# Sums kept in banks over turned token orders, last queries moved, maxima by trees, norm sums by stationary ones

## The chip, the cores and the metric

The kernel runs on one core of one Trainium2 chip. The metric is the device time of the program in microseconds (us), the median of several runs. The profile is one further execution of the same program under the hardware profiler. The engines are named as the profile names them: PE is TensorE with its matmuls, PEld its weight loads, DVE is VectorE, ACT is ScalarE, POOL is GpSimd and SP is SyncE, whose queue issues the transfers.

## The reference

Three stages follow one another. `attn` has 4 batches of 8 heads with 576 tokens of 64 values, and 32 memory slots for each head:

```python
a = phi - np.max(phi, axis=2, keepdims=True)           # over the 576 tokens
a = np.exp(a); a = a / (np.sum(a, axis=2, keepdims=True) + 1e-09)
k_m = np.einsum('bhsm,bhsd->bhmd', a, k)
v_m = np.einsum('bhsm,bhsd->bhmd', a, v)
scores = scale * np.matmul(q, k_m.transpose(0, 1, 3, 2))
scores = scores - np.max(scores, axis=-1, keepdims=True)
attn = np.exp(scores); attn = attn / (np.sum(attn, axis=-1, keepdims=True) + 1e-09)
attn_out = np.matmul(attn, v_m)
...
x = attn_out.transpose(0, 2, 1, 3).reshape(2304, 512)
h = x @ w_in                                           # 512 -> 2048
x = (h * (1.0 / (1.0 + np.exp(-1.702 * h)))) @ w_out   # 2048 -> 512
...
rms = np.sqrt(np.mean(x * x, axis=-1, keepdims=True) + 1e-06)
xn = x / rms * rms_g
g = xn @ w_gate                                        # 512 -> 1536
out = (g * (1.0 / (1.0 + np.exp(-g))) * (xn @ w_val)) @ w_o2
```

## The kernel before, in words

**Passes.** The 2304 tokens go in two passes `pr` of two batches, 1152 tokens each. Tokens lie along the columns of the tiles and model channels along the 128 partitions, so x of a pass is `x2[pr]`, four tiles `e` of 128 channels by 1152 tokens (the profile calls them x_0 and x_1). Nearly every product is made of three matmuls on a high and a low part of each factor (names that end in h and l, or index 0 and 1 of a pair).

**Attention.** A unit is a batch with half of its heads. Its steps are `att_k1` (maximum of phi over the tokens, by one reduction on DVE) or `att_k1t` (the same by a tree of `tensor_tensor` maxima; batches 0 and 1 use it), `att_k2` to `att_k5` (exp, sums, `k_m` and `v_m`; `att_k3s` sums the exponentials), then `att_q1` to `att_q4` (scores, their maxima, exponentials and sums, and `attnT`). Batch 0 is laid out on 128 partitions, the others on 96; the stage tile of batch 0 is padded by a memset of 1152 columns.

**First MLP.** The hidden 2048 channels go in 8 groups `g` of 256 (`a_g1`, `a_g2`). `vm_part` multiplies `v_m` by the group's slice of `w_in` beforehand (tiles vm_0 to vm_3, two banks apiece); `a_g1` multiplies `attnT` by it, 288 tokens at a time (pg<-attnT,vm_3h), ACT applies the activation and POOL or DVE forms the low part (gr). `a_g2` multiplies by `w_out` (pg<-gr,a_outh), for a token tile `t` and each `e`, six matmuls into one PSUM bank. DVE then adds the bank to x2: x<-x,pg. The token tiles are 384 wide, and 288 wide only in the first two groups of the first pass. All groups run their tokens in rising order.

**Norm.** Per pass and per tile of 384 tokens: `norm_1` squares and adds on ACT and POOL (sq, then sr); `norm_2` sums over the channels by six matmuls of 128 columns with the squares as weights (bank pnm), takes a root of 3 columns on ACT and a reciprocal of 3 columns on DVE; `norm_3` spreads these over the partitions by three transposes (bank pnr) and an ACT copy to rb; `norm_4` multiplies the four tiles of x by rb and rg on DVE.

**Second MLP.** `s_g3` and `s_g4` make the three products by sums and differences of quarters, group b for the first pass and s for the second (tiles ps_A, ps_S, c, oacc). The first pass's norm and its part b are spread over the second pass of the first MLP, its tokens over the slots of that pass.

**What sets the order.** The steps are not issued where they are called. A class `Plan` records every operation, and a list scheduler inside it gives each engine its queue, with estimated costs (`cost`), due times (shifted for some steps by a table `HASTE`) and a table `OTHER` that names operations to move between DVE and POOL. Where it expects the PE to stand still before a matmul that takes a new bank, `fill` puts matmuls of the constant `ones_r` (512 or 128 columns) into that bank first, which are overwritten. `plan.issue` emits everything from one line, so the profile shows L644 for nearly all instructions. PSUM has 8 banks of 512 values for each partition (pool `ps`), shared by all uses.

```python
    def issue(self, tc):
        with tc.manual_schedule():
            for _, _, op in self.order():
                getattr(self.real[op.eng], op.name)(*op.args, **op.kw)
...
    kmiscp = pool("kmi", 1, strict=True)
    psp = pool("ps", 8, bass.MemoryType.PSUM, spare=2, ahead=4)
```

Of the kernel before, what the change touches and what calls it, by code (L numbers as in the profile page):

```python
# [10 lines left out]
F32 = mybir.dt.float32  # L11
# [105 lines left out]
class Plan:  # L117
# [12 lines left out]
        "a_g1 0 0 1": 19.4,  # L130
        "a_g1 0 1 1": 11.5,
        "a_g1 0 1 2": 21.4,
        "a_g1 0 3 0": 26.4,
        "a_g1 0 4 0": 21.9,
        "a_g1 0 5 0": 26.3,
        "a_g2 0 0 2": 16.5,
        "a_g2 0 0 3": 13.2,
        "a_g2 0 1 0": 9.5,
        "a_g2 0 2 0": 23.0,
        "a_g2 0 2 2": 27.6,  # L140
        "a_g2 1 5 1": 110.4,
        "att_k1 2 1": 45.4,
        "att_k2 2 1": 35.4,
        "att_k3 0 0": 96.8,
        "att_k5 0 1": 60.2,
        "att_k5 2 0": 7.8,
        "att_q1 2 1 0": 0.3,
        "att_q3 1 0 0": 43.2,
        "att_q3 1 0 1": 81.5,
        "att_q3s 2 1 0": 3.9,  # L150
        "att_q3s 2 1 1": 35.9,
        "att_q3s 3 0 0": 35.4,
        "att_q3s 3 0 1": 59.0,
        "att_q4 1 1 0": 43.7,
        "att_q4 2 0 0": 22.2,
        "att_q4 2 1 1": 4.4,
        "att_q4 3 1 1": 69.4,
        "ld_src 0 0 1": 71.5,
# [5 lines left out]
        "s_g3 0 7 2": 67.1,
        "s_g3 1 0 2": 116.4,
        "s_g3 1 11 1": 57.9,
        "s_g3 1 11 2": -61.0,
        "s_g4 0 0 5": 45.2,
        "s_g4 0 0 6": 52.3,
        "s_g4 0 1 4": 58.8,  # L170
        "s_g4 0 5 5": 80.4,
        "s_g4 1 4 2": 131.2,
        "s_g4 1 5 0": -73.1,
        "t_a 0 1": 70.9,
        "t_b 0 1": 59.7,
        "t_c 0 0": 31.9,
        "t_d 0 1": 42.8,
        "vm_part 0 5 0": 29.8,
        "w_conv a 0 0 in 1": 62.2,
        "w_conv c 5 gate 1": 36.4,  # L180
        "w_conv c 5 o2 0": 48.2,
        "w_load a 0 0 in 1": 81.8,
        "w_load a 0 1 out 1": 56.9,
        "w_load a 0 4 out 1": 55.7,
        "w_load a 0 5 in 1": 66.5,
        "w_load b 1 vg": 141.7,
        "w_load c 2 val 1": 115.6,
        "w_load c 3 val 0": 126.6,
# [208 lines left out]
    def cost(op):  # L397
# [17 lines left out]
        if op.eng == "POOL":  # L415
            two = op.name == "tensor_tensor"
            each = 0.00215 if two else 0.00104 if op.kw.get("op0") is ALU.mult else 0.00355
            if op.kw.get("op") is ALU.mult:
                each = 0.0016
            t = 0.05 + each * n + (0.1 if two else 0.0)  # L420
            return t, t + 0.05
# [226 lines left out]
def kernel(  # L648
# [285 lines left out]
    def ld_src(u, i):  # L934
        b, g = u
        x = (k, v, q)[i][b, 4 * g : 4 * g + 4]
        if u not in stage:
            stage[u] = big(f"stage{b}_{g}")
            if b < N9:
                V.memset(stage[u][:, 3456:4608], 0.0)  # L940
# [383 lines left out]
    def a_g1(pr, g, t):  # L1324
# [23 lines left out]
        if t == 3:  # L1348
            vm.pop((pr, g))
            if g == NA - 1:  # L1350
                attnT.pop(pr)

    def a_g2(pr, g, t, eng=A):
        w = width(pr, g)
        n = slice(t * w, (t + 1) * w)
        if pr not in x2:
            x2[pr] = big(f"x2_{pr}").rearrange("p (e n) -> p e n", e=NE)
# [3 lines left out]
        for e in range(NE):  # L1361
            es = slice(e * P, (e + 1) * P)
            ps = psum("pg2")
            i = 0
            for fc in range(2):
                for a, y in ((0, 0), (1, 0), (0, 1)):
                    PE.matmul(
                        ps[:, :w], lhsT=wo[a][:, fc, es], rhs=gr[fc][:, y, :w],
                        start=(i == 0), stop=(i == 5),
                    )  # L1370
                    i += 1
            if g == 0:
# [5 lines left out]
        if t == PT // w - 1:  # L1378
# [20 lines left out]
    def norm_2(pr, t):  # L1399
        sr = nrm.pop((pr, t))  # L1400
        ps = psum("pnm")
        for s in range(TB // P):
            c = slice(s * P, (s + 1) * P)
            for y in range(2):
                PE.matmul(
                    ps[:, c], lhsT=sr[:, y, c], rhs=ones_r, start=(y == 0), stop=(y == 1)
                )
        r = smp.tile([P, 2, 4], F32, tag="r", name="r")
        A.activation(
# [413 lines left out]
```

## Time and profile before

| | us |
|---|---|
| median of 3 runs | 847.02 (846.75 to 849.77) |
| the profiled execution, whole | 843.96 |
| the profiled execution, span of its trace | 842.2 |
| PE busy in the span | 827.5 (98%) |
| DVE busy | 655.1 (78%) |
| ACT busy | 494.0 (59%) |
| POOL busy | 296.4 (35%) |

The span runs from the first to the last recorded instruction; 1.76 us of the execution lie around it. The profiled execution is 3.06 us shorter than the median of the timed runs. A share of busy time is a mean over the whole span, and stages differ: DVE is busy nearly all the time in the first pass and less than half of it at the end.

### The profile page before, as it was taken

Reading aid. Unit: us, or ns where it says so; the run is one execution under the profiler, and the core shown is the slowest. Engines: PE = TensorE matmul, PEld = TensorE weight load, DVE = VectorE, ACT = ScalarE, POOL = GpSimd, SP = SyncE. Lnnn points to the kernel's source line nnn. Section 1 sums busy time; section 2 is a strip of 40 time slices with the busy share of each in tenths; the row PEclk is TensorE's granted clock in tenths of the full one; section 3 lists DMA queues with packets and bytes.
Section 4 is the critical chain, followed back from the end, with each engine's and each line's share of the span. In section 5 each row is a group of like instructions: output and inputs, shape, how many; then the busy total and the mean of one; then the engine's idle time right before and its main releaser. Section 6 shows DMA issues by size and latency. Waiting matters only on the chain.

```text
span 842.2 us, 16000 instructions
## 1 busy us (share of the span) xinstructions
PE 827.5 (98%) x5789; PEld 787.4 (93%) x5789; DVE 655.1 (78%) x1363; ACT 494.0 (59%) x1222; POOL 296.4 (35%) x295
## 2 busy tenths in 40 slices
PE   7999999999999999999999999999999999999997
PEld 6899999999999999999999999999999999999996
DVE  7978999999998998989989888767775435545555
ACT  4687878687778757666577755435552443323321
POOL 4444555666344556455846510120450000000000
PEclk9989999999999999999999999999999999999999
DMA  9964757856848776665676478463455543514314
GB/s 340 271 214 144 236 204 206 275 192 188 278 170 279 253 237 222 211 217 190 219 256 230 165 276 287 163 238 131 157 163 168 184 147 104 200 55 171 126 50 113
DMA packets 76767, 166.99 MB, mean 198 GB/s; under 512 B 7312, under 2 KB 29328, under 8 KB 76688
## 3 DMA queue, kind: packets, MB, share of 16 engines
q1 hardware_dynamic: 76688, 165.97, 59.5%
q8 instruction: 46, 0.75, 0.4%
q14 instruction: 33, 0.27, 0.1%
HBM read 106.69 MB, written 59.24 MB: 197 GB/s over the span
## 4 chain that ended last, share of the span: by engine, by line
PE 78%; DVE 10%; DMA 4%; issue 3%; ACT 3%; POOL 2%; SPq 0%; POOLq 0%; ACTq 0%; DVEq 0%
PE pg L644 42%; PE ps_A L644 21%; PE ps_S L644 9%; DVE pad L644 3%; PE pvm L644 2%; DVE x L644 2%; PE pq L644 2%; PE pk L644 1%; DMA stage<-in_q_dram 1%; DVE kmisc L644 1%; DVE stage L644 1%; DVE cv L644 1%; DMA stage<-in_v_dram 1%; DMA raw_c_gate<-in_moe_w_gate_dram 1%; DMA raw_a_out<-in_moe_w_out_dram 1%
## 5 line engine op out<-in xcount | busy, mean ns | idle before, releaser
L644 PE MATMUL pg<-gr,a_outh 128*128 128x384 f32 (+1 forms) x736 | 195.2, 334 | 0.8 <-POOL gr L644 0.6
L644 PEld LDWEIGHTS pg<-gr,a_outh 128*128 128x128 f32 x736 | 132.7, 188 | 2.4 <-POOL gr L644 2.0
L644 PE MATMUL pg<-gr,a_outl 128*128 128x384 f32 (+1 forms) x368 | 121.9, 331 | 0.0
L644 POOL TENSOR_TENSOR gr<-gf,gr 128x288 fp32r<-128x288 f32 (+2 forms) x118 | 83.8, 727 | 101.1 <-ACT gr L644 52.4
L644 PE MATMUL pg<-s_o,pp 128*128 128x512 f32 x432 | 114.0, 391 | 0.0
L644 ACT COPY c<-ps_A 128x320 f32<-128x320 f32 (+1 forms) x144 | 57.2, 399 | 93.7 <-PE ps_A L644 91.8
L644 DVE TENSOR_TENSOR x<-x,pg 128x384 f32<-128x384 f32 (+1 forms) x172 | 88.9, 535 | 11.0 <-PE pg L644 9.7
L644 DVE TENSOR_TENSOR oacc<-oacc,pg 128x512 f32<-128x512 f32 x90 | 61.7, 686 | 45.7 <-PE pg L644 44.9
L644 PEld LDWEIGHTS pg<-s_o,pp 128*128 128x128 f32 x432 | 79.0, 188 | 14.6
L644 PE MATMUL ps_A<-tba,s_A 128*128 128x320 f32 (+1 forms) x576 | 88.5, 296 | 0.0
L644 PEld LDWEIGHTS ps_A<-tba,s_A 128*128 128x128 f32 x576 | 81.9, 190 | 1.6
L644 DVE TENSOR_TENSOR c<-c,ps_S 128x320 f32<-128x320 f32 (+1 forms) x96 | 43.2, 452 | 37.6 <-PE ps_S L644 29.3
L644 PEld LDWEIGHTS pg<-gr,a_outl 128*128 128x128 f32 x368 | 69.1, 188 | 0.0
L644 ACT ACTIVATE gf<-pg 128x288 f32<-128x288 f32 x128 | 50.5, 412 | 31.1 <-PE pg L644 27.4
L644 ACT CAST gr<-gf 128x288 fp32r<-128x288 f32 (+2 forms) x184 | 59.2, 363 | 6.9 <-PE pg L644 4.3
L644 PE MATMUL pg<-s_o,tbd 128*128 128x512 f32 x216 | 61.1, 392 | 0.0
L644 DVE TENSOR_TENSOR c<-c 128x256 f32<-128x256 f32 (+1 forms) x86 | 39.3, 466 | 18.3 <-ACT c L644 16.6
L644 POOL TENSOR_SCALAR pad<-pad 128x512 f32<-128x512 f32 x20 | 41.2, 2062 | 19.9 <-ACT pad L644 19.7
L644 POOL TENSOR_SCALAR cv<-cv 128x512 f32<-128x512 f32 x20 | 44.1, 2210 | 8.1 <-ACT cv L644 6.5
L644 PE MATMUL ps_A<-tbc,s_S 128*128 128x256 f32 (+1 forms) x288 | 46.0, 297 | 0.0
L644 PE MATMUL ps_A<-tbd,s_A 128*128 128x320 f32 (+1 forms) x288 | 45.7, 297 | 0.1
L644 PE MATMUL ps_S<-tbb,s_S 128*128 128x256 f32 (+1 forms) x288 | 45.8, 296 | 0.0
(234 smaller groups left out, 1881.5 us busy)
## 6 DMA issues: line engine op xcount, KB each, us to landing
cache_s<-s_S SPq DMA_DIRECT2D x24, 512.0 KB, 3.7
s_S<-cache_s SPq DMA_DIRECT2D x24, 512.0 KB, 3.5
cache_b<-cv SPq DMA_DIRECT2D x36, 256.0 KB, 4.5
raw_a_in<-in_moe_w_in_dram SPq DMA_DIRECT2D x16, 512.0 KB, 5.3
raw_a_out<-in_moe_w_out_dram SPq DMA_DIRECT2D x16, 512.0 KB, 5.4
raw_c_gate<-in_moe_w_gate_dram SPq DMA_DIRECT2D x12, 512.0 KB, 4.7
raw_c_val<-in_moe_w_val_dram SPq DMA_DIRECT2D x12, 512.0 KB, 4.3
raw_c_o<-in_moe_w_out_dram SPq DMA_DIRECT2D x12, 512.0 KB, 4.4
```

Source lines behind the costliest of these rows:

```text
L644: getattr(self.real[op.eng], op.name)(*op.args, **op.kw)
```

## The change

Six edits come together. **Turned tokens and kept banks:** in the first MLP odd groups above 1 run their token tiles from 3 to 0 (`back`), so that two neighbouring groups meet at the same token tile. There the four banks of the earlier group are not closed, and the next group's matmuls add to them (`keeps`, `kept`); the four DVE additions of the earlier group go. **Half width in the second pass:** its first two groups also run 288 tokens at a time, slots `again`. **Queries of the last batch:** `att_steps` becomes `att_k` and `att_q`, and `att_q` of batch 3 runs at the start of the second pass (`last_side`). **Trees:** all units take `att_k1t`, and `att_k3s` goes to G (POOL). **Norm:** `norm_2` uses `ones_r` as the weights and the squares as the moving side, so that every partition holds the sums at once; root and reciprocal work on 384 columns, and `norm_3` is gone. **Memset:** the padding of the stage tile moves to POOL, with a cost for it in the planner. The tables `HASTE` and `OTHER` are replaced as a whole.

```diff
     HASTE = {
-        "a_g1 0 0 1": 19.4,
...
+        "a_g1 1 2 0": 114.4,
...
     OTHER = {
-        "a_g1 0 0 0": (17,),
...
+        "a_g1 0 0 0": (8,),
...
-                V.memset(stage[u][:, 3456:4608], 0.0)
+                G.memset(stage[u][:, 3456:4608], 0.0)
...
-    gt, x2 = {}, {}
+    gt, x2, kept, fresh = {}, {}, {}, set()
+    KEPT = range(NE)
+
+    def back(pr, g):
+
+        return g % 2 and g > 1
+
+    def keeps(pr, g, e):
+
+        return 1 < g < NA - 1 and e in KEPT
 
     def width(pr, g):
-        return HALF if (pr, g) in ((0, 0), (0, 1)) else TB
+        return HALF if g < 2 else TB
...
+        last = 0 if back(pr, g) else PT // w - 1
...
-            ps = psum("pg2")
-            i = 0
+            ps = kept.pop((pr, g, t, e), None)
+            i, keep = 0 if ps is None else 1, t == last and keeps(pr, g, e)
+            ps = psum("pg2") if ps is None else ps
             for fc in range(2):
                 for a, y in ((0, 0), (1, 0), (0, 1)):
                     PE.matmul(
                         ps[:, :w], lhsT=wo[a][:, fc, es], rhs=gr[fc][:, y, :w],
-                        start=(i == 0), stop=(i == 5),
+                        start=(i == 0), stop=(fc == 1 and (a, y) == (0, 1) and not keep),
                     )
                     i += 1
-            if g == 0:
+            if keep:
+                kept[pr, g + 1, t, e] = ps
+                fresh.add((pr, t, e)) if g == 0 else None
+            elif g == 0 or (pr, t, e) in fresh:
+                fresh.discard((pr, t, e))
                 copy(eng, acc[:, e, n], ps[:, :w])
...
     def norm_2(pr, t):
         sr = nrm.pop((pr, t))
         ps = psum("pnm")
-        for s in range(TB // P):
-            c = slice(s * P, (s + 1) * P)
-            for y in range(2):
-                PE.matmul(
-                    ps[:, c], lhsT=sr[:, y, c], rhs=ones_r, start=(y == 0), stop=(y == 1)
-                )
-        r = smp.tile([P, 2, 4], F32, tag="r", name="r")
-        A.activation(
-            out=r[:, 0, 0:3], in_=ps[:, 0:TB:P], func=AF.Sqrt, bias=epst, scale=1.0 / DM
-        )
-        V.reciprocal(out=r[:, 1, 0:3], in_=r[:, 0, 0:3])
-        nrm[pr, t] = r
-
-    def norm_3(pr, t):
...
-        A.copy(out=nrm[pr, t], in_=ps[:, :TB])
+        for y in range(2):
+            PE.matmul(ps[:, :TB], lhsT=ones_r, rhs=sr[:, y], start=(y == 0), stop=(y == 1))
+        r = kmiscp.tile([P, 1024], F32, tag="kmi", name="rb")
+        A.activation(out=r[:, :TB], in_=ps[:, :TB], func=AF.Sqrt, bias=epst, scale=1.0 / DM)
+        V.reciprocal(out=r[:, TB : 2 * TB], in_=r[:, :TB])
+        nrm[pr, t] = r[:, TB : 2 * TB]
...
-    def att_steps(u, k3, k3s, q1, q3s):
-        if u[0] < 2:
-            yield att_k1t, u, V
-        else:
-            yield att_k1, u
+    def att_k(u, k3):
+        yield att_k1t, u, V
         yield att_k2, u
         yield att_k3, u, k3
         if u[0] >= N9:
-            yield att_k3s, u, k3s
+            yield att_k3s, u, G
         yield att_k4, u
         yield att_k5, u
+
+    def att_q(u, q1, q3s):
...
+    def last_side():
+        for g in range(2):
+            yield from att_q((3, g), (A, A), (G, G))
...
-            side, per = pair_side(0), 1
+            side, per = last_side(), 2
...
-            line(a_g1, *key[1:], t)
+            turned = back(*key[1:])
+            line(a_g1, *key[1:], 3 - t if turned else t)
```

What the planner makes of it shows at two places. The first is DVE in the second pass of the first MLP, where the first norms of x_0 are made. Before, a norm's reciprocal has 3 columns (r) and stands between the low parts of vm_2:

```order
L644 TENSOR_TENSOR x_1_702<-x_1_702,pg_757 128x384
L644 TENSOR_TENSOR vm_2l<-pvm,vm_2h 64x256 x3
L644 RECIPROCAL r<-r 128x3
L644 TENSOR_TENSOR vm_2l<-pvm,vm_2h 64x256
L644 TENSOR_TENSOR gr<-gf,gr 128x192
```

In the changed kernel two reciprocals of 384 columns (rb) stand in the same queue, one ahead of the squares of the third token tile (sq_0_2), one between the low parts of vm_3:

```order
L605 RECIPROCAL rb<-rb 128x384
L605 TENSOR_TENSOR sq_0_2_790<-sq_0_2_790 128x384
L605 SCALAR_TENSOR_TENSOR x_0_211<-x_0_211,rg,rb 128x384 x2
L605 TENSOR_TENSOR x_1_661<-x_1_661,pg_781 128x288
L605 SCALAR_TENSOR_TENSOR x_0_211<-x_0_211,rg,rb 128x384 x2
L605 TENSOR_TENSOR x_1_661<-x_1_661,pg_809 128x384
L605 TENSOR_TENSOR vm_3l<-pvm,vm_3h 64x2x256
L605 RECIPROCAL rb<-rb 128x384
L605 TENSOR_TENSOR vm_3l<-pvm,vm_3h 64x2x256
L605 SCALAR_TENSOR_TENSOR x_0_211<-x_0_211,rg,rb 128x384 x3
L605 TENSOR_TENSOR x_1_661<-x_1_661,pg_810 128x384
L605 SCALAR_TENSOR_TENSOR x_0_211<-x_0_211,rg,rb 128x384
```

The reciprocal, its width and the multiplications by rb have moved ahead of vm_3l, whose last four pieces come in the row behind these. The second place is PE at the start, in the attention of batches 0 and 1 (stage_0, stage_1; pq are its banks, pvm those of vm_part). Before, the fills with ones_r go into a bank of vm_part:

```order
L644 MATMUL pk_217<-ident,mx 96x128
L644 MATMUL pq_140<-twin,stage_0_115 128x64 x3
L644 MATMUL pvm<-ones_r 128x512 x9
L644 MATMUL pvm<-ones_r 128x128 x2
L644 MATMUL pvm<-wide,vlh_131 128x256
```

In the changed kernel they stand ahead of the scores' transposes of batch 0 (pq_140), and ahead of the sums of batch 1 (pk_190):

```order
L605 MATMUL pq_153<-stage_1_117 64x2x32 x4
L605 MATMUL pq_153<-stage_1_117 64x32 x4
L605 MATMUL pq_140<-ones_r 128x512 x18
L605 MATMUL pq_140<-ones_r 128x128
L605 MATMUL pq_140<-twin,stage_0_115 128x64 x3
L605 MATMUL pk_190<-ones_r 128x512 x2
L605 MATMUL pk_190<-ones_r 128x128
```

Nineteen fills now precede pq_140, and the matmuls of vm_part (wide) have left this place.

## Rows read from the trace of the kernel before

**Rows 1.** The page: the span and the busy time by engine.

```profile
span 842.2 us, 16000 instructions
PE 827.5 (98%) x5789; PEld 787.4 (93%) x5789; DVE 655.1 (78%) x1363; ACT 494.0 (59%) x1222; POOL 296.4 (35%) x295
```

**Rows 2.** Windows: stretch, length, busy PE, PEld, DVE, ACT, POOL; clock; DMA.

```profile
0.00:47.00 47.00, 40.30 (x402) 35.30 (x403) 38.12 (x99) 28.33 (x69) 19.17 (x27) 0.94 1.01 312
40.00:50.00 10.00, 9.03 (x55) 8.74 (x56) 6.60 (x19) 6.45 (x19) 4.64 (x4) 0.66 0.99 295
60.00:240.00 180.00, 177.84 (x1421) 172.18 (x1421) 169.87 (x351) 138.53 (x338) 96.14 (x91) 1.00 0.69 223
240.00:411.00 171.00, 170.21 (x1113) 169.33 (x1112) 155.74 (x302) 117.37 (x288) 96.48 (x100) 1.00 0.66 218
411.00:490.00 79.00, 78.86 (x523) 74.53 (x522) 69.19 (x130) 56.59 (x125) 47.33 (x42) 1.00 0.60 204
```

**Rows 3.** Timeline of PE: start, length of a run of instructions, what it is.

```profile
282.09 0.34 PE L644 MATMUL pg<-gr,a_outh 128*128 128x384 f32 x1
282.27 0.49 PE L644 MATMUL pnr<-ident,r 128*128 128x128 f32 x3
282.51 0.42 PE L644 MATMUL pg<-gr,a_outh 128*128 128x384 f32 x1
...
428.32 0.78 PE L644 MATMUL pnm<-ones_r,sr 128*128 128x128 f32 x6
428.94 1.81 PE L644 MATMUL ps_A<-tbd,s_A 128*128 128x320 f32 x12
```

**Rows 4.** Groups on DVE by form: busy us, mean ns | idle before, releaser.

```profile
L644 DVE TENSOR_TENSOR x<-x,pg 128x384 f32<-128x384 f32 x156 | 81.8, 544 | 9.6 <-PE pg L644 8.4
L644 DVE SCALAR_TENSOR_TENSOR x<-x,rg,rb 128x384 f32<-128x384 f32 x24 | 15.6, 680 | 0.5 <-ACT rb L644 0.5
L644 DVE TENSOR_REDUCE kmisc<-kmisc 96x128 f32<-96x768 f32 x8 | 12.1, 1518 | 0.0
L644 DVE TENSOR_TENSOR x<-x,pg 128x288 f32<-128x288 f32 x16 | 7.1, 448 | 1.4 <-PE pg L644 1.3
L644 DVE TENSOR_TENSOR y<-kmisc 96x384 f32<-96x384 f32 x3 | 2.3, 759 | 0.0
L644 DVE TENSOR_TENSOR kmisc<-kmisc,y 96x128 f32<-96x128 f32 x3 | 0.9, 284 | 0.0
L644 DVE MEMSET stage<- 128x1152 f32 x2 | 2.0, 1018 | 0.3 <-issue 0.2
L644 DVE RECIPROCAL r<-r 128x3 f32<-128x3 f32 x6 | 0.9, 168 | 0.8 <-ACT r L644 0.8
L644 DVE RECIPROCAL stage<-stage 128x12 f32<-128x12 f32 x2 | 0.5, 228 | 0.3
```

**Rows 5.** Groups on POOL by form.

```profile
L644 POOL TENSOR_SCALAR pad<-pad 128x512 f32<-128x512 f32 x20 | 41.2, 2062 | 19.9 <-ACT pad L644 19.7
L644 POOL MEMSET kz<- 128x192 f32 x8 | 2.3, 282 | 7.9 <-PE pk L644 7.9
```

**Rows 6.** What PE waited for, by window: us in total, times, longest.

```profile
PE pvm L644 <- DVE a_inl L644: 0.8, 1, 0.8
...
PE pg L644 <- POOL gr L644: 0.6, 1, 0.6
PE pnr L644 <- DVE r L644: 0.2, 1, 0.2
```

**Rows 7.** Timeline of PE at the start.

```profile
33.18 2.38 PE L644 MATMUL pvm<-ones_r 128*128 128x512 f32 x11
...
47.01 0.83 PE L644 MATMUL pg<-attnT,vm_0h 128*128 128x288 f32 x2
...
55.58 0.42 PE L644 MATMUL pg<-gr,a_outh 128*128 128x288 f32 x2
55.84 0.29 PE L644 MATMUL pg<-gr,a_outl 128*128 128x288 f32 x1
```

More of the change, by code (lines that the diff above doesn't have):

```diff
@@ L129 @@
     HASTE = {
-        "a_g1 0 0 1": 19.4,
[L131 to L146, printed above, removed]
@@ L164 @@
[L164 to L180, printed above, removed]
@@ L181 @@
[L181 to L188, printed above, removed]
+        "a_g1 1 2 0": 114.4,
+        "a_g2 0 1 1": 112.8,
+        "a_g2 0 1 2": 93.7,
+        "a_g2 0 3 1": 53.1,
+        "a_g2 0 3 2": 61.7,
+        "a_g2 0 4 0": 39.7,
+        "a_g2 1 6 0": 122.4,
+        "a_g2 1 7 0": 106.9,
@@ new lines @@
+        "att_q1 2 1 1": 84.7,
+        "att_q3 1 0 1": 314.7,
+        "att_q3 2 1 0": 60.8,
+        "att_q3 3 0 1": 174.3,
+        "ld_phi 0 1": 652.0,
+        "norm_4 0 2 2": 123.4,
+        "norm_4 0 2 3": 132.3,
+        "s_g3 0 11 2": 194.1,
+        "s_g4 1 2 2": 222.6,
+        "s_g4 1 5 4": 243.3,
+        "s_g4 1 5 5": 95.7,
+        "s_g4 1 5 6": 95.0,
+        "s_g4 1 5 8": 77.2,
+        "t_b 0 0": 53.9,
+        "t_b 0 1": -44.6,
+        "t_c 0 0": 31.4,
+        "vm_part 0 1 0": 124.4,
@@ L189 @@
+        "w_conv a 0 6 in 0": 82.9,
+        "w_conv c 1 o2 1": 100.3,
+        "w_conv c 5 val 0": 133.4,
     }
     OTHER = {
[1 row of a table removed]
[1 row of a table added]
         "a_g1 0 0 2": (8,),
[12 rows of a table removed]
[10 rows of a table added]
         "a_g1 0 4 0": (17,),
[3 rows of a table removed]
[3 rows of a table added]
         "a_g1 0 5 2": (19, 21),
[19 rows of a table removed]
[20 rows of a table added]
         "a_g1 1 4 2": (8, 10, 19, 21),
[3 rows of a table removed]
[2 rows of a table added]
         "a_g1 1 5 3": (17,),
[3 rows of a table removed]
[6 rows of a table added]
         "att_k3 1 0": (2,),
@@ L416, in cost @@
             two = op.name == "tensor_tensor"
-            each = 0.00215 if two else 0.00104 if op.kw.get("op0") is ALU.mult else 0.00355
+            each = 0.00215 if two else 0.00104 if op.name == "memset" or op.kw.get("op0") is ALU.mult else 0.00355
             if op.kw.get("op") is ALU.mult:
@@ L1347, in a_g1 @@
                 sub_lo(G, gr[:, 1, d], gf[:, c0:c1], gr[:, 0, d])
-        if t == 3:
+        if t == (0 if back(pr, g) else 3):
             vm.pop((pr, g))
@@ L1377, in a_g2 @@
                 )
-        if t == PT // w - 1:
+        if t == last:
             wt.pop(("a", pr, g, "out"))
@@ L1401, in norm_2 @@
         ps = psum("pnm")
-        for s in range(TB // P):
-            c = slice(s * P, (s + 1) * P)
-            for y in range(2):
-                PE.matmul(
-                    ps[:, c], lhsT=sr[:, y, c], rhs=ones_r, start=(y == 0), stop=(y == 1)
-                )
-        r = smp.tile([P, 2, 4], F32, tag="r", name="r")
-        A.activation(
-            out=r[:, 0, 0:3], in_=ps[:, 0:TB:P], func=AF.Sqrt, bias=epst, scale=1.0 / DM
-        )
-        V.reciprocal(out=r[:, 1, 0:3], in_=r[:, 0, 0:3])
-        nrm[pr, t] = r
-    def norm_3(pr, t):
-        r = nrm.pop((pr, t))
-        ps = psum("pnr")
-        for s in range(TB // P):
-            PE.transpose(
-                ps[:, s * P : (s + 1) * P], r[:, 1, s : s + 1].to_broadcast([P, P]), ident
-            )
-        nrm[pr, t] = kmiscp.tile([P, 1024], F32, tag="kmi", name="rb")[:, :TB]
-        A.copy(out=nrm[pr, t], in_=ps[:, :TB])
+        for y in range(2):
[4 more added lines that the diff above has]
+        nrm[pr, t] = r[:, TB : 2 * TB]
     def norm_4(pr, t, e):
@@ L1622, in do @@
         at(*step)
-        plan.keen = step[0] in (norm_1, norm_2, norm_3, norm_4)
+        plan.keen = step[0] in (norm_1, norm_2, norm_4)
         step[0](*step[1:])
@@ L1653, in att_side @@
             yield ld_unit, u
-            yield from att_steps(u, G, V, (A, A), (G, G))
+            yield from att_k(u, G)
+            if u[0] == 2:
+                yield from att_q(u, (A, A), (G, G))
+    def last_side():
+        for g in range(2):
+            yield from att_q((3, g), (A, A), (G, G))
     def norm_side(pr):
@@ L1674, in weights, with unit @@
         conv(hf)
-    def unit(u, k3, q3s):
-        for step in att_steps(u, k3, G, (A, A, A) if u[0] < N9 else (A, A), q3s):
+    def unit(u, k3, q3s=None):
+        for step in att_k(u, k3) if k3 else att_q(u, (A, A, A) if u[0] < N9 else (A, A), q3s):
             do(step)
     first = [("a", 0, g, t) for t2 in (0, 2) for g in range(2) for t in (t2, t2 + 1)]
+    again = [("a", 1, *x[2:]) for x in first]
     slots = first + [
@@ L1684 @@
         for key in groups[2:]
+        if key not in (("a", 1, 0), ("a", 1, 1))
         for t in range(4 if key[0] == "a" else 3)
     ]
+    j1 = 4 * NA
+    slots[j1:j1] = again
     at_slot = {0: halves(groups[1])[:2], 1: halves(groups[1])[2:]}
@@ L1691 @@
             continue
-        nxt = halves(groups[2] if j < 8 else groups[i + 1])
+        nxt = halves(groups[2] if j < 8 else groups[NA + 2] if j1 + 4 <= j < j1 + 8 else groups[i + 1])
         if key[0] == "a":
-            at_slot.setdefault(j, []).extend(nxt[j % 4 : j % 4 + 1])
+            if j1 <= j < j1 + 2:
+                nxt = halves(groups[NA + 1])
+                at_slot.setdefault(j, []).extend(nxt[2 * (j - j1) : 2 * (j - j1) + 2])
+            elif not j1 + 2 <= j < j1 + 4:
+                at_slot.setdefault(j, []).extend(nxt[j % 4 : j % 4 + 1])
             if key[1]:
-                at_slot[j] += [later.pop(0)]
+                at_slot.setdefault(j, []).append(later.pop(0))
         else:
@@ L1716 @@
     for g in range(2):
-        unit((0, g), V, (G, G))
+        unit((0, g), V)
+        unit((0, g), None, (G, G))
     for hf in outs:
@@ L1733 @@
             for g in range(2):
-                unit((1, g), G, (G, G))
-            for g in range(2):
-                for c in range(2):
-                    line(vm_part, 0, g, c, 1)
+                unit((1, g), None, (G, G))
+            for c in range(2):
+                line(vm_part, 0, 0, c, 1)
             side = att_side()
+        if j == j1 + 4:
+            for step in side:
+                do(step)
+            side, per = pair_side(0), 2
         if key == ("a", 1, 0) and t == 0:
@@ L1747 @@
             if pr:
-                for step in islice(pair_side(1), 7 * NTB, None):
+                for step in islice(pair_side(1), 6 * NTB, None):
                     do(step)
@@ L1759 @@
         if j == 1:
+            for g in range(2):
+                unit((1, g), G)
+        if j in (1, j1 + 1):
             for c in range(2):
-                line(vm_part, 0, 1, c, 0)
-        nxt = groups[2] if j == 6 else groups[i + 1] if j > 7 and t == 2 and i + 1 < len(groups) else None
+                line(vm_part, j // j1, 1, c)
+        nxt = groups[2] if j == 6 else groups[NA + 2] if j == j1 + 6 else None if j1 <= j < j1 + 8 else groups[i + 1] if j > 7 and t == 2 and i + 1 < len(groups) else None
         if nxt and nxt[0] == "a":
@@ L1782 @@
         elif t:
-            late = [(a_g2, *key[1:], t - 1)]
+            late = [(a_g2, *key[1:], 3 - t if turned else t - 1)]
         for step in islice(side, per + (j % 4 == 1) if j else 0):
```

18 lines of the change are left out of this document (removed), and 214 rows, old and new, of the table OTHER.

## The prediction

> **What bounds the kernel now.** I read the page first. PE is busy for 827.5 of 842.2 us, every other engine for less than four fifths [rows 1]. The time can therefore fall in two ways only: PE gets fewer or shorter instructions, or the 14.7 us in which it stands still shrink. The windows say where these are. From 0 to 47 us, attention ahead of the first `a_g1`, PE is busy 40.30 of 47.00; from 60 to 240 us, the first pass of the first MLP, it misses 2.16; from 240 to 411, the second pass, 0.79; from 411 to 490, the start of part b, 0.14 [rows 2]. The rest lies in the tail, which the change does not touch. The same windows show who is near the bound behind PE: DVE, busy 169.87 of 180 us in the first pass, 155.74 of 171 in the second, 69.19 of 79 in b. The view of waits names what PE waited for longest: in the first pass a low part made by DVE (0.8 us), in the second a low part by POOL (0.6 us) and the norm's r by DVE (0.2 us) [rows 6]. So a microsecond less of DVE is not a microsecond of time; in the first pass at most the 2.16 us can be had.
>
> One stretch has another limit. Between 40 and 50 us the granted clock is 0.66, a mean of the two levels 1.2 and 2.4 GHz, while it is 1.00 in all windows from 60 us on [rows 2]. PE had been feeding itself fills at 33.18 [rows 7] and then took short matmuls with waits between them. What a full clock would give there is at most (1 − 0.66) × 10 = 3.4 us.
>
> **The norm's matmuls.** I take distances between starts as the price, since matmuls overlap. Six pnm matmuls take 428.94 − 428.32 = 0.62 us, three pnr transposes 282.51 − 282.27 = 0.24 [rows 3]: 0.86 for each norm. The new form is two matmuls of 384 columns; one takes 282.27 − 282.09 = 0.18 [rows 3], so 0.36. Six norms save 6 × 0.50 = 3.0 us of PE work, and the wait of 0.2 us for r goes with the transposes: **−3.2**. This is work on the bounding engine, which nothing can hide; I take ± 0.5.
>
> **Fewer additions.** A kept group boundary saves four DVE additions; there are five in each pass, so 20 × 0.544 = 10.9 us [rows 4] in each. The trees replace 8 reductions of 1518 ns by 24 `tensor_tensor`; with 759 + 284 and one more of about 284 that is 1.33 us against 1.52 [rows 4], 1.5 us less in all. Batch 3's queries leave the first pass. With the mean of each group of the trace for every instruction of the queue, DVE's work between the first and the last addition to x_0 goes from 176 to 159 us. Over some 180 us that is a share of 0.88, below the 0.91 (155.74 of 171) at which the second pass misses only 0.79. Of the 2.16 us that PE misses I take **−2.0** (bounds 0, if the misses are POOL's, and −2.2). With it go the fills that the planner had put into a late bank of batch 3, two of 512 columns and one of 128; eleven fills take 2.38 us at the start [rows 7], so **−0.5** (0 to −1).
>
> The kept banks have a price that no row shows: from the last token tile of a group to the first of the next, four of the eight banks are held, and `a_g1` runs on the others. If PE then waited each time as it waited once for gr, 0.6 us [rows 6], ten boundaries would cost 6 us. The banks' readers, ACT's activations and DVE's additions, follow PE closely and DVE has fewer additions just there, so I take 0 (0 to +6).
>
> **Half width.** In the second pass 144 matmuls of 384 columns become 192 of 288, equally many columns. Two of 288 take 55.84 − 55.58 = 0.26 [rows 7], so 192 × 0.13 = 25.0 against 144 × 0.18 = 25.9. I take **+0.3** (−0.9 to +0.7, for 48 more instructions and weight loads). The 16 more additions cost DVE 16 × 0.448 us [rows 4] and 12 of 0.544 go.
>
> **The start.** Two memsets of 1.02 us leave DVE [rows 4]. On POOL one takes longer: 282 ns for 192 columns [rows 5], so some 1.7 us for 1152, and the two stand in the queue in which each pad costs 2.06 us [rows 5]. `att_q` of batch 1 and part of `vm_part` move behind the first `a_g1`. Nineteen fills stand ahead of pq_140; eleven took 2.38 us before [rows 7], so these take about 4. They delay nothing that is ready, but show where the planner expects PE to wait, and for POOL. Against the 6.7 us missed and the fills that are there now [rows 2, 7], I take **−1** (−5, if the half clock goes too, to +3, if POOL is late).
>
> **The reciprocals.** Six `reciprocal` of 3 columns at 168 ns become six of 384 columns. The trace has none so wide. From 3 to 12 columns the time goes from 168 to 228 ns [rows 4], 6.7 ns a column; carried on to 384 that is 0.168 + 381 × 0.0067 = 2.7 us. From below, an addition of 384 columns takes 0.544 [rows 4], and a reciprocal won't be faster. Between them I take the slope, rounded to 2.5, because it is measured on the operation itself. The order shows what stands behind: in the second pass one lies ahead of the squares of the third tile, so the third pnm comes later; the next lies amid the low parts vm_3l, and with seven multiplications of 0.68 us behind it [rows 4], so the last vm_3l, which the `a_g1` of the group's turn wants, comes some 2 × 2.3 = 4.6 us later. DVE's work in the second pass, by the same sum as above, goes from 154 to 161 and with three reciprocals to 168 us, while PE's part grows by some 5 us that it loses in the first pass (the moved queries). That makes DVE as busy as it was in the first pass before, where PE missed 2.16. I take **+3** (0 if the reciprocal is short or covered, +7 if all of the delay shows). In b three more lie within a stretch in which DVE has 79 − 69.19 = 9.8 us free [rows 2] and needs 3 × 2.3 = 7 of them: **+0.7** (0 to +4).
>
> The Trainium skill, page "VectorE: DVE Perf Modes", section "First, the fixed hardware budget", says that Reciprocal is an iterative divide with a repeat count of 8; at the 0.96 GHz of its "Specifications" that would be, as an estimate, 8.3 ns a column and 3.2 us for 384. The sum would be about 1 us worse by it in the second pass and 1 us in b. The measured slope of 6.7 ns stands nearer to that than to one column a cycle.
>
> **Sum.** −3.2 − 2.0 − 0.5 + 0.3 − 1.0 + 3.0 + 0.7 = −2.7 us, so the profiled 843.96 would become 841.3. The median of the runs is 847.02, 3.06 us above the profiled one; I put the same difference on the median: 844.3, rounded to **844**. Half a per cent, 4.2 us, is about what a measurement can tell from no change; the likeliest case is inside of it.
>
> **Rivals.**
> - *The reciprocal is covered or short.* PE loses nothing for it, so the +3.0 and the +0.7 fall out: 847.0 − 6.4 = 840.6. For it speaks that only 0.79 us are missed in the second pass now, and that a planner with due times may have left room; against it, 155.74 of 171 us of DVE.
> - *The start gains as well.* The half clock at 40 to 50 us goes (−3.4) on top of that or of a part of it: 836 to 838. For it, fills stand ahead of pq_140 and keep PE going; against it, more work for POOL at a place where PE waits.
> - *No change that can be told.* The additions were all hidden, and the norm's 3 us are given back by the reciprocals or the held banks: 846.5 to 848.
> - *Slower: the reciprocals.* At 2.5 us six cost DVE 14 us more. If all six stand in PE's way, the sum is −6.4 + 14 = +7.6, or 854.6; with five sixths of it, 852. It ends on the slower side of no change once more than 6.4 us of the 14 show, and of 0.5% once 10.6 do. For it speaks that three stand in the second pass ahead of work that PE wants within the same group, and three in b with 9.8 us free; against it, that b's first matmuls can go on with the token tiles already normed.
>
> **Chances.** The sum's own case, 840.5 to 847.5, has 0.36; the covered reciprocal 0.22; the start as well 0.11; no change 0.15; slower 0.16. Faster than 842.8 are the second and third, and about a fifth of the first: 0.40. Slower than 851.2 is most of the last and a little for held banks: 0.17. Within it 0.43. The range leaves out the lower part of the start's case and the upper one of the reciprocals': 836.5 to 851.5. The sum's own range is 840.5 to 847.5.
>
> **What would show it.** The reciprocals of rb have a row with their mean: 2.5 us by me; below 1 us the first rival holds. PE's view of waits in the second pass should name DVE, at vm_3l, or the third pnm, with 1 to 4 us; if POOL's gr or DVE's x appear at the turns of groups, the held banks are the cost. pnm must show 12 matmuls of 384 columns 0.18 apart and no pnr. PE's missing time from 60 us to the end of the first pass should fall below 1 us; if it stays at 2, DVE was not what PE waited for. The first `a_g1` against 47.01 and the clock between 40 and 50 us tell of the start. Wrong I would be if the second pass and b lose more than 8 us, or if the start moves by more than 4.

## The result, and the profile after

The changed kernel takes 856.28 us (median of 5 runs, 852.9 to 857.45) against 846.75 us of the kernel before beside it: 1.0098 times as long, 95% interval 1.0071 to 1.0124. It is slower by 9.5 us; 844 and no measurable change were forecast, and the range ended at 851.5. The profiled execution took 857.45 us, 13.5 more than that of before. The two profiles lie at opposite ends: before's is 3.06 us below its median, the changed kernel's is the longest of its five, so they show about 4 us more of a loss than the medians do.

The page of the changed kernel, which answers to [rows 1]:

```profile
span 855.6 us, 15960 instructions
PE 831.6 (97%) x5799; PEld 788.3 (92%) x5799; DVE 659.0 (77%) x1372; ACT 489.4 (57%) x1204; POOL 261.4 (31%) x256
```

PE is busy 4 us longer in a span 13.4 us longer. The windows of the stretches of [rows 2], with the same columns:

```profile
60.00:240.00 180.00, 175.20 (x1389) 170.22 (x1389) 165.21 (x342) 132.37 (x332) 92.74 (x95) 1.00 0.67 214
240.00:411.00 171.00, 165.55 (x1138) 162.47 (x1137) 156.97 (x301) 117.18 (x282) 80.65 (x72) 1.00 0.64 215
411.00:490.00 79.00, 75.41 (x481) 71.68 (x480) 64.74 (x120) 52.83 (x116) 37.00 (x40) 0.98 0.63 209
```

PE misses 4.80, 5.45 and 3.59 us, 13.84 in all, where it missed 2.16, 0.79 and 0.14, 3.09 in all. That is 10.75 of the 13.4 us by which the span grew; the first product with vm_0 comes 2.26 us later, at 49.27 instead of 47.01. What PE waited for, from the view of waits of these three stretches (us in total, times, longest):

```profile
PE pg L605 <- ACT gf L605: 1.9, 3, 1.0
PE pk L605 <- DVE kmisc L605: 1.1, 1, 1.1
...
PE pg L605 <- ACT gf L605: 2.0, 3, 1.3
PE pg L605 <- DVE vm_3l L605: 1.6, 1, 1.6
PE pnm L605 <- POOL sr L605: 0.9, 1, 0.9
...
PE ps_S L605 <- DVE c L605: 1.2, 1, 1.2
PE ps_A L605 <- ACT s_S L605: 1.2, 1, 1.2
PE ps_A L605 <- POOL s_A L605: 0.7, 1, 0.7
```

(The names s_A, s_S and c are sums and differences that part b multiplies; sr is the sum of squares that pnm takes.) Two things are new. Products into pg wait for gf, ACT's activation that frees a bank, in both passes. And in the second pass and b, PE waits for work that stands behind DVE's reciprocals. Their group on DVE by form, beside the additions that answer to [rows 4]:

```profile
L605 DVE TENSOR_TENSOR x<-x,pg 128x384 f32<-128x384 f32 x104 | 54.8, 546 | 5.2 <-PE pg L605 4.7
L605 DVE RECIPROCAL rb<-rb 128x384 f32<-128x384 f32 x6 | 15.3, 2547 | 0.7 <-ACT rb L605 0.6
```

52 additions of 384 columns are gone, 16 of 288 have come with the half width, and six reciprocals of 2.55 us. DVE's timeline at the second of them:

```profile
308.56 2.54 DVE L605 RECIPROCAL rb<-rb 128x384 f32<-128x384 f32 x1
311.02 0.62 DVE L605 TENSOR_TENSOR vm_3l<-pvm,vm_3h 64x512 fp32r<-64x512 f32 x1
311.56 1.66 DVE L605 SCALAR_TENSOR_TENSOR x<-x,rg,rb 128x384 f32<-128x384 f32 x3
313.15 0.54 DVE L605 TENSOR_TENSOR x<-x,pg 128x384 f32<-128x384 f32 x1
313.61 0.61 DVE L605 SCALAR_TENSOR_TENSOR x<-x,rg,rb 128x384 f32<-128x384 f32 x1
314.25 1.45 DVE L605 TENSOR_TENSOR vm_3l<-pvm,vm_3h 64x256 fp32r<-64x256 f32 x4
```

and PE's at the same place, the products that need vm_3l:

```profile
312.68 0.48 PE L605 MATMUL pg<-attnT,vm_3h 128*128 128x288 f32 x2
314.73 0.75 PE L605 MATMUL pg<-attnT,vm_3l 128*128 128x288 f32 x2 [1.57 <-DVE vm_3l L605]
```

DVE hardly rests from 308.56 to 315.7; PE has its first two products done at 313.16 and stands until the first piece of the last vm_3l. Part b's DVE, at the last two reciprocals:

```profile
466.23 2.55 DVE L605 RECIPROCAL rb<-rb 128x384 f32<-128x384 f32 x1
468.82 2.21 DVE L605 SCALAR_TENSOR_TENSOR x<-x,rg,rb 128x384 f32<-128x384 f32 x4
470.94 0.42 DVE L605 TENSOR_TENSOR pp<-c,pp 128x256 fp32r<-128x256 f32 x1
471.74 2.55 DVE L605 RECIPROCAL rb<-rb 128x384 f32<-128x384 f32 x1 [0.37 <-ACT rb L605]
```

The norm takes nearly all of DVE's time from 466.23 to 474.3. PE's waits for s_A and s_S come between 473 and 482 in its timeline. Its granted clock falls amid them: it is 0.74 from 480 to 485 us, a mean of the two levels (1.2 and 2.4 GHz), and was 1.00 in the whole stretch before:

```profile
480.00:485.00 5.00, 3.88 (x19) 3.62 (x20) 4.00 (x4) 4.22 (x10) 4.11 (x5) 0.74 0.42 128
```

### The profile page after: what moved, and what is told of

The parts are those of the page before. It is cut to its first block, busy times and chain, and to the rows that moved or that the text cites. A ratio compares the mean times of both kernels' runs of the same rounds, so it can differ in the third digit from the quotient of the medians.

```text
span 855.6 us, 15960 instructions
## 1 busy us (share of the span) xinstructions
PE 831.6 (97%) x5799; PEld 788.3 (92%) x5799; DVE 659.0 (77%) x1372; ACT 489.4 (57%) x1204; POOL 261.4 (31%) x256
## 4 chain that ended last, share of the span: by engine, by line
PE 73%; DVE 10%; ACT 6%; DMA 4%; POOL 3%; issue 3%; SPq 0%; POOLq 0%; ACTq 0%; DVEq 0%
PE pg L605 39%; PE ps_A L605 20%; PE ps_S L605 9%; PE pq L605 3%; DVE x L605 2%; DVE pad L605 2%; PE pvm L605 2%; PE pk L605 2%; DMA raw_c_val<-in_moe_w_val_dram 1%; DVE cv L605 1%; DMA kmisc<-in_phi_dram 1%; ACT stage L605 1%; DVE rb L605 1%; ACT gf L605 1%; DMA stage<-in_v_dram 1%
## 5 line engine op out<-in xcount | busy, mean ns | idle before, releaser
L605 PEld LDWEIGHTS pg<-gr,a_outh 128*128 128x128 f32 x768 | 136.6, 188 | 4.3 <-ACT gf L605 1.5
L605 POOL TENSOR_TENSOR gr<-gf,gr 128x288 fp32r<-128x288 f32 (+2 forms) x95 | 76.8, 821 | 113.2 <-ACT gr L605 92.7
L605 ACT COPY c<-ps_A 128x256 f32<-128x256 f32 (+1 forms) x144 | 57.3, 399 | 83.1 <-PE ps_A L605 75.3
L605 PE MATMUL ps_A<-tba,s_A 128*128 128x256 f32 (+1 forms) x576 | 89.8, 296 | 0.7 <-POOL s_A L605 0.7
L605 DVE TENSOR_TENSOR x<-x,pg 128x384 f32<-128x384 f32 (+1 forms) x136 | 68.6, 523 | 6.9 <-PE pg L605 6.2
L605 POOL TENSOR_TENSOR pp<-c,pp 128x192 fp32r<-128x192 f32 (+4 forms) x12 | 7.3, 621 | 189.1 <-ACT pp L605 187.4
L605 PE MATMUL ps_A<-tbb,s_S 128*128 128x320 f32 (+1 forms) x288 | 45.6, 299 | 1.6 <-ACT s_S L605 1.2
L605 ACT CAST pp<-c 128x320 fp32r<-128x320 f32 (+4 forms) x96 | 30.3, 353 | 28.3 <-DVE c L605 14.8
L605 PE MATMUL ps_S<-tbc,s_S 128*128 128x320 f32 (+1 forms) x288 | 44.8, 296 | 1.2 <-DVE c L605 1.2
L605 PE MATMUL ps_S<-tbb,s_S 128*128 128x320 f32 (+1 forms) x288 | 46.0, 299 | 0.0
```

## The experiments

Most of them keep the order of instructions on every engine exactly as the planner made it, and change single instructions as they are issued. A new search of the order would bring differences of its own. The diffs give what each edit comes to in the kernel's lines, shortened. The kernel before was timed beside each group of them: 846.95, 846.93, 847.68 and 846.65 us.

**Short reciprocals.** The suspect alone:

```diff
-    V.reciprocal(out=r[:, TB : 2 * TB], in_=r[:, :TB])
+    V.tensor_copy(out=r[:, TB : 2 * TB], in_=r[:, :TB])
```

> The changed kernel with its order of instructions kept as it is on every engine; only the six reciprocals of 384 columns (2.55 us each) are replaced by DVE copies of 384 columns (an estimate from additions of that size: below 0.55 us), so x is multiplied by the root and not divided by it. If the reciprocals' length is what the second pass and part b lose, the waits for vm_3l, sr and for c, s_S and s_A in b go, and the time falls by 5 to 9 us below the changed kernel, to 847 to 851. If the order itself or the held banks are to blame, it falls by less than 3 us.

Measured: 845.55 us, 0.9980 of before (0.9958 to 1.0003), so 10.7 us less than the changed kernel, more than the 5 to 9 expected, and not to be told from before. A copy takes 422 ns, so the six shortened DVE's queue by 6 × (2.547 − 0.422) = 12.75 us, and 84% of that showed in the time. The windows of this run, same stretches:

```profile
60.00:240.00 180.00, 176.02 (x1387) 171.00 (x1386) 165.98 (x343) 131.73 (x329) 92.17 (x92) 1.00 0.68 221
240.00:411.00 171.00, 170.08 (x1178) 168.94 (x1177) 156.83 (x311) 121.28 (x292) 81.40 (x77) 1.00 0.66 224
411.00:490.00 79.00, 78.36 (x517) 74.28 (x516) 66.23 (x128) 55.25 (x122) 37.18 (x38) 1.00 0.67 226
```

PE misses 0.92 and 0.64 in the second pass and b, where the changed kernel missed 5.45 and 3.59. The first pass, where no norm is made, still misses 3.98, more than before. The waits for gf in the first and the second pass are

```profile
PE pg L608 <- ACT gf L608: 1.3, 2, 1.1
...
PE pg L608 <- ACT gf L608: 0.3, 1, 0.3
```

with all banks held as before. So of the 2.0 us for gf in the second pass most went with the reciprocals' length.

**Banks closed.** No bank is held; 40 additions come back:

```diff
+    last matmul of a kept bank: stop=True
+    V.tensor_tensor(out=acc[:, e, n], in0=acc[:, e, n], in1=ps[:, :w], op=ALU.add)
+    next group: a bank of its own, start=True
```

> The changed kernel with its order kept, but no bank is held over a group's end: each of the 40 banks is closed, a DVE addition to x follows 0.5 us after its last matmul in DVE's order, and the next group takes a new bank. If the held banks starve the products with vm, the waits of PE for gf (six, 3.9 us in all in the changed kernel's profile) go and the time falls by 3 to 5 us, although DVE has 40 additions more (22 us). If the additions saved are worth more than the banks, the time rises by 2 to 6 us.

Measured: 864.26 us, 1.0212 (1.0192 to 1.0233): 8.0 us more than the changed kernel, above the 2 to 6 expected. Waits of PE in the first and the second pass:

```profile
PE pg L617 <- DVE gr L617: 1.7, 2, 1.0
...
PE pg L617 <- DVE vm_7l L617: 2.0, 1, 2.0
PE pg L617 <- POOL gr L617: 1.7, 3, 0.7
```

The waits for gf are gone in the first pass and 0.7 us in the second, so held banks had a part in them; in the second pass they make long waits only together with the long reciprocals, since either edit takes most of them away. Low parts (gr, vm_7l) are late in their place. In this order the held banks save more than they cost.

**Both.** 

> Both of the edits before at once, order kept: copies in the place of the six reciprocals (the division by the root is left out), and banks closed at each group's end. If both theories hold and add, 8 to 13 us below the changed kernel, 843 to 848; if the 40 additions fill the room that the short reciprocals leave, no better than the short reciprocals alone.

Measured: 855.34 us, 1.0102 (1.0083 to 1.0121). The two nearly add: 8.9 us less than with the banks closed alone, where the copies took off 10.7. My expectation of a gain from each was wrong for the banks: with copies, closing them costs 9.8 us.

**Early table.** One exponential of a column of zeros ahead of everything on ACT:

```diff
+    nc.vector.memset(warmt, 0.0)
+    nc.scalar.activation(out=warmt, in_=warmt, func=AF.Exp)
     plan.issue(tc)
```

> The changed kernel with one more ACT instruction at the start, an exponential of one column of zeros, so that ACT's first table is loaded before phi arrives; all else as it was. In the changed kernel the first exponentials start at 10.60 us, 1.28 of it a table load behind DVE's kmisc, against 7.92 before. If the start hangs on them, the first products of k (13.41) come 1.2 us earlier and so does the first product with vm_0 (49.27), and the time falls by about 1.2 us. If a transfer or POOL sets the start, the first product with vm_0 does not move by more than 0.4.

ACT's timeline at the start, first of the changed kernel:

```profile
9.31 1.28 ACT L605 ACT_TABLE_LOAD   x1 [9.31 <-DVE kmisc L605]
10.60 2.76 ACT L605 ACTIVATE stage<-kmisc 64x576 f32<-64x576 f32 x4
```

and with the early exponential:

```profile
0.71 1.28 ACT L1771 ACT_TABLE_LOAD   x1 [0.71 <-PEq L1790]
...
8.55 2.76 ACT L605 ACTIVATE stage<-kmisc 64x576 f32<-64x576 f32 x4 [6.29 <-DVE kmisc L605]
```

Measured: 855.21 us, 1.0103 (1.0086 to 1.0120), 1.1 us less than the changed kernel's median, about as expected but within the two intervals. The first products of k come at 11.37 instead of 13.41 us and the first product with vm_0 at 47.35 instead of 49.27, which lies within what profiles of the changed order differ by (46.20 to 50.43, see below).

**The kernel before with long reciprocals.** The reverse of the first:

```diff
+    for _ in range(2):
+        V.reciprocal(out=spare, in_=r[:, 0, 0:1].to_broadcast([128, 192]))
     V.reciprocal(out=r[:, 1, 0:3], in_=r[:, 0, 0:3])
```

> The kernel before, its order kept, with two reciprocals of 192 columns (each about 1.3 us, an estimate from 2.55 us for 384) of the root, into a tile that nothing reads, just ahead of each of the six reciprocals of 3 columns. If six times 2.6 us on DVE in the place of the norm's reciprocal cost PE most of their length wherever they stand, 852 to 860. If it was the changed kernel's order that gave DVE no room, and before had some, below 850.

Measured: 870.11 us, 1.0272 (1.0231 to 1.0313), above both bounds: 23 us for 12 reciprocals of 1.35 us, 16.2 us of DVE. Here PE's transposes need r itself. Its waits in the second pass, and from 411 to 520 us:

```profile
PE pnr L648 <- DVE r L648: 7.3, 3, 2.9
...
PE pnr L648 <- DVE r L648: 6.6, 3, 2.4
```

13.9 us are such waits. Of the other 9, most is the clock's by an estimate: its mean in the second pass and in the stretch to 490 us is 0.97 and 0.98, where it was 1.00 before, and (1 − 0.97) × 171 + (1 − 0.98) × 79 = 6.7.

```profile
240.00:411.00 171.00, 163.71 (x1053) 162.85 (x1053) 151.19 (x288) 112.09 (x276) 84.85 (x91) 0.97 0.63 206
411.00:490.00 79.00, 74.21 (x475) 71.00 (x475) 69.79 (x123) 50.09 (x110) 48.96 (x43) 0.98 0.65 216
```

The rest I can't place. Because the edit makes PE's own way to r longer, it doesn't tell whether DVE's queue before had room for a long instruction elsewhere.

**Reciprocal root on ACT.** One activation in the place of root and reciprocal:

```diff
-    A.activation(out=r[:, :TB], in_=ps[:, :TB], func=AF.Sqrt, bias=epst, scale=1.0 / DM)
-    V.reciprocal(out=r[:, TB : 2 * TB], in_=r[:, :TB])
+    A.activation(out=r[:, TB : 2 * TB], in_=ps[:, :TB], func=AF.Abs_reciprocal_sqrt, bias=epst, scale=1.0 / DM)
```

> The changed kernel with its order kept, but ACT's root is made by one activation that gives the reciprocal root at once into the tile that DVE's reciprocal wrote, and the six reciprocals are gone. If only their length on DVE counts, it is as fast as the copies in their place or up to 1 us faster, 843 to 846; if ACT loads more tables for it or is late, 846 to 850.

Measured: 845.87 us, 0.9979 (0.9957 to 1.0002), as the copies. Its group on ACT:

```profile
L609 ACT ACTIVATE rb<-pnm,epst 128x384 f32<-128x384 f32 x6 | 3.5, 582 | 0.1
```

582 ns is what the root alone took in the changed kernel. So the division costs ACT no time here, and the gain is that of the copies although x is divided by the root.

**Logarithm and exponential on ACT.** The same with two activations:

```diff
-    A.activation(..., func=AF.Sqrt, ...); V.reciprocal(...)
+    A.activation(..., func=AF.Ln, ...); A.activation(..., func=AF.Exp, scale=-0.5)
```

> The changed kernel with its order kept, but ACT makes a logarithm in the place of the root and then, where DVE's reciprocal stood, an exponential of minus half of it: six more ACT instructions and eight more table loads of 1.28 us each on ACT (10 us), six reciprocals fewer on DVE. If DVE's time alone counts, 844 to 848; if the table loads delay the activations that PE waits for, 848 to 855.

Measured: 857.97 us, 1.0124 (1.0088 to 1.0159), above both ranges. In the second pass PE waits 2.9 us at once for an activation, and in b

```profile
PE ps_A L611 <- ACT s_A L611: 2.8, 1, 2.8
```

Ahead of both, ACT's queue has two table loads of 1.28 us with one activation between them; they hold PE up as a reciprocal on DVE does.

**No fills.** All `Fill` matmuls left out. 

> The changed kernel with its order kept and all 61 fills with ones_r left out. If the fills lie in time in which PE has nothing to do and keep its clock up, the time does not fall, and rises by 2 to 8 us with a granted clock near 0.5 in more of the first 60 us. If the fills stand in the way (19 ahead of pq_140, and fills at half clock), the first product with vm_0 comes 1 to 3 us earlier and the time falls by as much.

Measured: 864.14 us, 1.0202 (1.0171 to 1.0233), 7.9 us more. The window of the first 60 us (clock after the five busy times) and the first product with vm_0:

```profile
0.00:60.00 60.00, 42.54 (x368) 38.41 (x369) 39.12 (x105) 29.64 (x70) 24.74 (x31) 0.74 0.90 284
56.08 0.83 PE L607 MATMUL pg<-attnT,vm_0h 128*128 128x288 f32 x2
```

The granted clock is 0.74 on the mean against 0.91 with fills, and the product comes at 56.08 instead of 49.27. The fills don't stand in the way.

**The norm edit alone, in the order of before.** With the reciprocal root on ACT, first where ACT copied pnr to rb:

```diff
-    pnm: six matmuls of 128 columns; pnr: three transposes; A.activation(r, Sqrt); V.reciprocal(r); A.copy(rb, pnr)
+    pnm: two matmuls of 384 columns; A.activation(rb, pnm, Abs_reciprocal_sqrt) in the place of A.copy
```

> The kernel before, its order kept, with the norm edit alone and without its cost on DVE: in the place of the first pair of pnm matmuls two matmuls of 384 columns with ones_r as weights, no transposes, and where ACT copied pnr to rb one activation that gives the reciprocal root from the bank; no reciprocal. If the norm's matmuls are worth what their spacing says (0.86 against 0.36 us, six times) and the wait for r of 0.2 us goes, 3 us less than before: 843.5 to 844.5. If PE's time there is covered or ACT's longer activation makes it wait, within 1 us of before.

Measured: 853.26 us (847.45 to 855.68), 1.0054 (1.0031 to 1.0077): slower, outside both ranges. ACT's timeline at PE's longest wait in b:

```profile
435.50 1.28 ACT L646 ACT_TABLE_LOAD   x1
436.80 0.58 ACT L646 ACTIVATE rb<-pnm,epst 128x384 f32<-128x384 f32 x1
437.27 0.45 ACT L646 CAST tbd<-c 128x320 fp32r<-128x320 f32 x1
437.73 1.28 ACT L646 ACT_TABLE_LOAD   x1
439.02 0.47 ACT L646 ACTIVATE c<-c 128x320 f32<-128x320 f32 x1
```

Away from the root's place it loads its table and the next one again, and PE waits 2.9 us for c. A second run made the edit in the root's place, where no table load is added (28, as in before; the text below has 22, which is the changed kernel's number):

> The kernel before, its order kept, with the norm edit alone, like the run that made the reciprocal root where ACT copied pnr, but with the activation in the place of the root, next to the table load that the root already needed; ACT's queue then has 22 table loads again and a root's 3 columns become 384. If PE's saved 0.5 us a norm are worth their length, and that run lost them to table loads in part b (the 2.9 us in which PE waited for c), 3 us less than before: 843.5 to 845. If the saved matmuls lie beside other waits, within 1 us of before.

Measured: 853.30 us, 1.0070 (1.0050 to 1.0090). From 411 to 490 us:

```profile
411.00:490.00 79.00, 74.36 (x473) 69.81 (x472) 64.20 (x119) 54.22 (x116) 42.53 (x40) 0.98 0.64 214
```

PE misses 4.64 instead of 0.14, 2.9 of it for c again, so the table loads of the first run were not the whole reason. ACT stands before that activation until DVE has made s_S:

```profile
437.39 1.28 ACT L648 ACT_TABLE_LOAD   x1 [2.33 <-DVE s_S L648]
```

The pool `kmi` of rb has one buffer, which the sums `s` use too, and s_S is made from them: written early, rb stands in ACT's queue until they are read, and c stands behind it. In this order the norm edit alone is slower. Whether its 3 us of matmuls would show without the wait for c is not shown.

**Fewer additions in the order of before.** 40 of x<-x,pg left out, 20 in each pass:

```diff
-    V.tensor_tensor(out=acc[:, e, n], in0=acc[:, e, n], in1=ps[:, :w], op=ALU.add)   # g > 2, one t of each
```

> The kernel before, its order kept, with 40 of the additions of banks to x2 left out (per pass, groups 3 to 7, one token tile each), so 11 us less of DVE in each pass and the sums incomplete. No bank is held. If PE's 2.2 us missed in the first pass were DVE's, as the prediction took it, 2 us or more less: 843 to 845. If they were POOL's, ACT's and the transfers', within 1 us of before.

Measured: 846.49 us, 0.9992 (0.9973 to 1.0011): no change that can be told, between 2.3 us less and 0.9 more. In the first pass DVE is busy 165.93 us, 3.9 less and not the 11 of the twenty additions, since other work falls into the stretch and some of it takes longer; in the second pass it is 10.1 less. PE misses 1.69 in the first pass instead of 2.16:

```profile
60.00:240.00 180.00, 178.31 (x1437) 172.87 (x1436) 165.93 (x337) 140.98 (x350) 96.48 (x94) 1.00 0.66 216
```

**Reciprocal root and early table together.** 

> The changed kernel, order kept, with the reciprocal root on ACT (no reciprocal on DVE) and the exponential's table loaded early, both in one. If the two add, 1 us below the reciprocal root alone: 844 to 845.5, so 0.998 to 0.996 of before. If the start's length is set elsewhere, as after 845 to 847.

Measured: 843.24 us (12 runs, 840.87 to 848.88), 0.9948 of before (0.9929 to 0.9967). This is a little below what was expected, and faster than both kernels: by 0.5% than before beside it, by 1.5% than the changed kernel's median. It is 2.6 us less than the reciprocal root alone; the two intervals overlap. The first product with vm_0 is the earliest of all profiles:

```profile
44.79 0.48 PE L611 MATMUL pg<-attnT,vm_0h 128*128 128x288 f32 x2
```

**New tables.** The reciprocal root known to the planner, HASTE and OTHER searched anew for it:

> The changed kernel with the reciprocal root on ACT known to the planner and tables HASTE and OTHER searched anew for it, so another order on every engine. If the order was spoilt by a reciprocal that the planner took for a short one, 840 to 844. If the order is as good as it was and the rest of the change gives no more, 844 to 848.

Measured: 849.33 us, 1.0010 (0.9992 to 1.0028), above both ranges and 3.5 us more than the order kept. By this one search, the order that had been planned around a short reciprocal is no worse once the reciprocal is short.

## Why the prediction was wrong

**The step that failed is the reciprocals' share on PE's path.** Their length was forecast as 2.5 us and measured as 2.547, and the two places and the wait for vm_3l (1 to 4 us forecast, 1.57 measured) were those named. But I took +3 us in the second pass and +0.7 in b, 3.7 in all; the run with copies shows 10.7. What came was the rival "slower: the reciprocals", which wanted more than 6.4 of 14 us to show and five sixths for 852; 84% of 12.75 showed.

In the second pass I had read PE's loss off DVE's share of busy time (as busy as the first pass before, where PE missed 2.16), in b off 9.8 us of free time against a need of 7. Neither looks at how long a single free piece is. In the trace of before, DVE's 15.3 free us in the second pass lie in 67 pieces, 64 of them of 1.00 us or less and the longest of 2.42; the 9.8 in b lie in 26, the longest of 1.45. An instruction of 2.5 us fits in none, and what is queued behind it moves: in the second pass seven multiplications and the last pieces of vm_3l. The planner did not see it either: its `cost` gives such a reciprocal 0.075 + 384 / 960 = 0.475 us. An order planned with the true length was not tested.

The sign of being wrong that I had set, a loss of more than 8 us in the second pass and b, came true: 9.04 us are missed there, 0.93 before. DVE's busy time in b even fell, from 69.19 to 64.74 of 79 us, while PE missed 3.5 us more and its granted clock fell from 1.00 to 0.98.

The Trainium skill's rule for the reciprocal ("VectorE: DVE Perf Modes", "First, the fixed hardware budget") gave the estimate of 3.2 us for 384 columns; the trace has 2.55, nearer to the 2.7 of the rows' slope.

**Fewer additions: −2.0 forecast, no gain that can be told.** With 40 additions less and all else kept, 0.9992. I had read the share of DVE in the first pass as the reason of the 2.16 us; the largest wait, for a_inl, did go in that run, but only 0.5 us of the misses with it. Nor did DVE's work fall as far as I had it: between the first and the last addition of the first pass it went from 176.2 us of 184.3 to 166.6 of 179.6, where I had 159. PE's misses, which I had below 1 us, rose. In the changed kernel the first pass misses 4.80, with short reciprocals 3.98. Against the −2.0 and −0.5 that is, by one profile each, 4.3 us of the 5 by which the rest of the sum was too good: without reciprocals I had 840.6, and 845.55 was measured. This is the second term that failed, and its cause stays open: which part of the new order these waits come from was not separated. Waits for gf are 1.9 us of them, 1.3 with short reciprocals.

**Held banks: 0 forecast (0 to +6).** PE waits 3.9 us for gf in the two passes, 1.6 with short reciprocals, so holding has a price above 0 and within the bounds. It is repaid: closing the banks costs 8 us in this order.

**The norm's matmuls: −3.2 (± 0.5).** The spacing is as forecast, from PE's timeline in b, and pnr is gone:

```profile
454.24 0.52 PE L605 MATMUL pnm<-sr,ones_r 128*128 128x384 f32 x2
454.60 1.05 PE L605 MATMUL ps_A<-tbc,s_S 128*128 128x320 f32 x6
```

0.36 us for a norm. But "which nothing can hide" was too much: in the order of before the edit alone loses 0.5 to 0.7%, with a wait of 2.9 us for c in each of the two runs. What it gives in the changed order was not measured by itself.

**The start: −1 (−5 to +3).** One profile is not enough for it. The first product with vm_0 came at 49.27, 46.22, 50.43, 49.01, 47.26 and 46.20 us in six profiles of the changed order, 48.1 on the mean, and at 47.01, 51.73, 51.74, 50.46 and 48.97 in five of the order of before, 50.0 on the mean. So the product comes about 2 us earlier, and the profile of before that I worked from was an early one. That this is time gained is not shown, since part of `vm_part` and the queries of batch 1 now stand behind it. The half clock did not go: in the changed kernel's profile the clock is 1.00 between 40 and 50 us, but 0.91 over the first 60, where it was 0.94 before. The half width, the trees, the moved queries and the memset were not tested by themselves.

## What to carry to other kernels

Before an instruction is widened on an engine that feeds the bounding one, look at what is queued behind it and how long that engine's single free pieces are: here 25 us of free time, in pieces of at most 2.42 us, left 84% of six instructions of 2.5 us to show. A busy share doesn't say what load is worth. Forty additions taken from an engine that is busy for 94% of a stretch brought no time that can be told, though the longest wait that named it went; forty put back into the changed order, with the banks closed, cost 8 us. Ask whether another engine's instruction already passes over the data: here the root on ACT could give the reciprocal in the same 582 ns.

## What the runs showed of the hardware

DVE's reciprocal takes 1.35 us for 192 columns and 2.55 for 384, 6.2 ns a column, where an addition of 384 takes 0.55. ACT's reciprocal root of 384 columns takes 582 ns, as its root does. A table load on ACT takes 1.28 us. The memset of 1152 columns on POOL took 1.10 us, where I had worked out 1.7 from one of 192. Executions of one order of instructions differ by up to 4 us at the start, with a granted clock over the first 47 us between 0.85 and 1.00 in the profiles of the changed order with fills. Where PE waited longest its granted clock fell as well: to 0.74 on the mean from 480 to 485 us in b of the changed kernel, and to 0.97 over the second pass with the long reciprocals in the order of before. By the estimate there, that adds to the waits about half of what they take.
